# Half slots of a routed expert layer: layer 1 as products of 480 and 240 columns, with its sums, casts and low parts staggered by a block

## The chip, the cores and the metric

The kernel runs on one core of one Trainium2 chip. The metric is device time in microseconds (us). Three runs of the kernel before took 746.63 to 747.06 us, the median is 746.89 us. The core's engines each work through a queue of their own: TensorE (PE, products), ScalarE (ACT), VectorE (DVE), GpSimd (POOL, here mostly indirect DMAs) and SyncE (SP, which issues the other DMAs). PSUM, where PE puts its sums, has eight banks of 512 columns.

## The reference, cut to what matters

The first part is attention with a sigmoid; the change does not touch it. The second part is a layer of eight experts, each token going to one of them:

```python
logits = x @ w_gate
e_idx = np.argmax(logits, axis=1)
...
for e in range(E):
    mask = e_idx == e
    h = np.maximum(x[mask] @ w1[e], 0.0)
    ye = h @ w2[e]
    out[mask] = gate_w[mask, None] * eom[mask, e, None] * ye
```

There are 3,584 tokens (N) of 768 values, w1 is 768 x 1,024 and w2 is 1,024 x 768 for each expert.

## The kernel before, in words

Attention runs first (`attention`), and its last third already prepares the experts. Then the tokens are worked through in *slots*, one expert to a slot. A full slot holds 448 tokens (TB), a half slot up to 240 (TM), for what is left of an expert. How many of each there are is known only when the kernel runs, so the later slots stand in branches. In the runs shown seven full slots and two half slots are done; the two half slots are the last work of the kernel.

Numbers are kept in float32 and split into a high part, which the cast to PE's format gives (`split`, ScalarE), and a low part, the difference (VectorE): x into xh and xl, w1 into wh and wl, w2 into w2h and w2l, h into hh and hl. Each product of two matrices is three products of parts: high by high, high by low, low by high.

A half slot (`slot` with n = 32 * 8, which is not TB) goes like this.

- *Layer 1* (`layer1`, `layer1_mm`) has eight blocks, f = 0 to 7, of 128 rows of h. In each, PE makes six triples of products (d = 0 to 5), every one of 240 columns: wh by xh, wh by xl, wl by xh (lines 467 to 469). All three add into one PSUM bank of `psh`, three banks in turn. Then ScalarE takes the ReLU as hh (line 496), and VectorE the low part hl (line 497).
- Beside layer 1, w2 is split (`split_w2`, blocks 1 to 4, two rows of 128 x 768 a time), and as w2 and w1 share the raw buffer `w1r`/`w2r`, the loads of the next expert's w1 follow it (`load_w1`, SP). The next slot's tokens are gathered by GpSimd (`gather_rows`, line 389), one gather a block.
- *Layer 2* (`layer2`) has four groups of 24 products of 384 columns (lines 518 to 520): i = 0 and 1 make the two halves of the first 128 tokens, in the tile `ys[0]`, i = 2 and 3 those of the other 112, in `ys[1]`. ScalarE scales a group's sums into the tile (line 525), and after i = 1 and i = 3 GpSimd scatters the tile's rows to `out` (`scatter`, line 562).
- Beside layer 2, the next slot's w1 is split in three pieces of 128 x 2,048 (`split_w1`), its x is transposed by VectorE (`turn_x`) and split (`split_x`), and its w2 loaded (`load_w2`, SP) into the place that w1's raw pieces leave.

The first half slot has more to do, as it follows a full slot, whose last two columns' sums still stand in PSUM (`self.left`). The generator `finish` takes care of them, a step at each `next`: it turns them back (`turn_back`, VectorE, lines 485, 486, 508), stores them by eight DMAs, loads the rows again as four tiles, scales these on ScalarE (line 555) and scatters them from GpSimd. So six scatters leave during the first half slot's layer 2: two tiles named plain, then ys[0], hb, rbuf, then ys[1].

What sets the order: each engine's queue holds its instructions in the order in which the code writes them down, and an instruction that waits holds up all behind it. Waits come from the tiles: whoever writes a tile waits for those that still read it, DMAs among them.

A full slot's products are 512, 384 and 448 columns wide (`products`): xh and xl lie side by side in `x2`, and the first product takes 64 columns of xl along with 448 of xh, into a bank 512 wide.

Of the kernel before, what the change touches and what calls it, by code (L numbers as in the profile page):

```python
# [12 lines left out]
AF = mybir.ActivationFunctionType  # L13
ALU = mybir.AluOpType
# [16 lines left out]
TB = 448  # L31
TM = 240
GB_, GM = TB // 32, -(-TM // 32)
# [19 lines left out]
def r32(ap):  # L53
    return ap.bitcast(F32)


class Kernel:
# [19 lines left out]
    def memory(self):  # L77
        self.rounded = self.pool("rounded").tile([128, ROUNDED // 4], F32R, name="rounded")
        self.plain = self.pool("plain").tile([128, PLAIN // 4], F32, name="plain")
        ps = self.pool("psum", space=PSUM).tile([128, 8, 512], F32, name="ps")  # L80
        self.ps_s = [ps[:, 0:2], ps[:, 2:4]]
        self.ps_o = [[ps[:, 4], ps[:, 5]], [ps[:, 6], ps[:, 7]]]
        self.ps_s2 = ps[:, 6:8]
        self.psh = [ps[:, i] for i in (0, 1, 2)]
        self.psy = [ps[:, i] for i in (4, 5, 3)]
        self.ps_step = ps[:, 3, 0:8]
        self.rot = {}
        self.beat = [None, None]
        self.hints = {2: [ET.Activation, ET.DVE, ET.Pool]}

        c = self.carve
        w = c(0, 3, 2, 2, DF)
        self.w1s = [[w[:, d // 2, a, d % 2] for d in range(6)] for a in range(2)]
        self.w1p = [[w[:, k, a] for k in range(3)] for a in range(2)]
        self.x2 = c(12 * DF * 4, 6, 2 * TB)
        self.xs = [self.x2[:, :, TB * i:TB * i + TB] for i in range(2)]
        self.slots_begun = 0

        self.w1r = c(0, 6, DF, dt=F32)
        self.w2r = c(0, 8, DM, dt=F32)  # L100
        self.xg = c(6 * DF * 4, GB_, Q4, dt=F32)
        self.xT = c(6 * DF * 4 + XG, 6, TB, dt=F32)
        self.yq = c(6 * DF * 4 + XG, GB_, Q4, dt=F32)
        self.xTm = c(6 * DF * 4 + XG, 6, 32 * GM, dt=F32)
        self.spare = c(6 * DF * 4 + GM * Q4 * 4, DM, dt=F32), c(6 * DF * 4 + XG + 6 * 32 * GM * 4, DM, dt=F32)
# [315 lines left out]
        self.split(self.w1r[:, d], self.w1s[0][d], self.w1s[1][d])  # L421

    def split_w2(self, k):
        for f in (2 * k, 2 * k + 1):
            h, l = (w[f // 6][:, f % 6].rearrange("p (c a x) -> p a c x", a=4, x=32) for w in (self.w2h, self.w2l))
            self.split(self.w2r[:, f].rearrange("p (a c x) -> p a c x", a=4, x=32), h, l)

    def w2_at(self, f, c):
        return self.w2h[f // 6][:, f % 6, c], self.w2l[f // 6][:, f % 6, c]
# [18 lines left out]

    def split_x(self, s, k):
        if s is not None:  # L450
            q, n = slice(2 * k, 2 * k + 2), 32 * s["lx"].shape[1]
            self.split((self.xT if n == TB else self.xTm)[:, q], self.xs[0][:, q, 0:n], self.xs[1][:, q, 0:n])

    def change_step(self, times=2):
        for _ in range(times):
            self.nc.tensor.matmul(self.ps_step, self.zero, self.zero[:, 0:8], start=True, stop=True)

    def layer1_mm(self, f, n):
        nc = self.nc
        ps = self.h_ps = self.take("h", self.psh)  # L460
        c = slice(128 * f, 128 * f + 128)
        (wh, wl), (xh, xl) = self.w1s, self.xs
        for d in range(6):
            if n == TB and self.joined:
                mm = self.products(ps, wh[d][:, c], wl[d][:, c], self.x2[:, d], d == 0, d == 5)
            else:
                nc.tensor.matmul(ps[:, 0:n], wh[d][:, c], xh[:, d, 0:n], start=(d == 0), stop=False)  # L467
                nc.tensor.matmul(ps[:, 0:n], wh[d][:, c], xl[:, d, 0:n], start=False, stop=False)  # L468
                mm = nc.tensor.matmul(ps[:, 0:n], wl[d][:, c], xh[:, d, 0:n], start=False, stop=(d == 5))  # L469
            if d == 2:  # L470
                self.beat[1] = mm.ins
# [16 lines left out]
    def layer1(self, f, n, begun=False):  # L488
        nc = self.nc
        if not begun:  # L490
            self.layer1_mm(f, n)
        if n == TB and self.joined:
            self.join(self.h_ps)
        ps = self.h_ps[:, 0:n]
        hh, hl = (h[:, f, 0:n] for h in self.hs)
        self.beat[0] = nc.scalar.activation(hh, ps, AF.Relu).ins  # L496
        nc.vector.scalar_tensor_tensor(hl, ps, 0.0, r32(hh), ALU.max, ALU.subtract)  # L497

    def layer2_turned(self, c):
        ps = self.take("y", self.psy)  # L500
        for f in range(8):
            wh, wl = self.w2_at(f, slice(128 * c, 128 * c + 128))
            self.products(ps, wh, wl, self.h2[:, f], f == 0, f == 7)
        return ps
# [65 lines left out]
    def slot(self, cur, nxt, side=None, begun=False, hint=None):  # L570
        nx = None
        if nxt is not None:
            nx, rows, sure = nxt() if callable(nxt) else nxt
            last = -(-nx["lx"].shape[1] // 2) - 1
        n = 32 * cur["lx"].shape[1]
        lag = 0 if self.left is not None or n == TB else 2
        fin = self.finish(n)
        next(fin, None)
        self.rot["y"] = 1
        for f in range(8):  # L580
            if begun and f == 1:
                self.change_step()
            self.layer1(f, TB if n == TB else TM, begun and f == 0)
            if nx is not None and n < TB:
                if f >= lag:
                    self.gather_rows(nx, f - lag, rows, 1)
                if f == 7 and lag == 0:
                    self.nc.gpsimd.drain()
            elif nx is not None and f <= last:
                self.gather_rows(nx, 2 * f, rows, 1)  # L590
                self.gather_rows(nx, 2 * f + 1, rows, 0)
                if f == last and not sure:
                    self.nc.gpsimd.drain()
            if f == 6 and n < TB:
                next(fin, None)
            if side is not None:
                next(side, None)
            if 1 <= f < 5:
                self.split_w2(f - 1)
                if f > 1:  # L600
                    self.load_w1(nx, f - 2)
        if lag == 0:
            for k in range(3):
                self.turn_x(nx, k)
        if n == TB:
            next(fin, None)
            self.layer2_columns(cur, nx, side, hint, fin)
            self.slots_begun += 1
            return nx
        ws = {0: (0, 1), 1: (2,)}  # L610
        for i in range(4):
            t = i // 2
            self.layer2(cur, t, i % 2, self.ys[t])
            if nx is not None:
                if lag and i == 0:
                    for g in range(8 - lag, 8):
                        self.gather_rows(nx, g, rows, g % 2)
                    self.nc.gpsimd.drain()  # L618
                for k in ws.get(i, ()):
                    self.split_w1(k)  # L620
                    for j in range(k, 4 if k == 2 else k + 1):
                        self.load_w2(nx, j)
                if lag and i == 0:
                    for k in range(3):
                        self.turn_x(nx, k)
                if i < 3:
                    self.split_x(nx, i)
            if i < 2:
                next(fin, None)
            if side is not None:  # L630
                next(side, None)
            if hint is not None and i == 1:
                self.tc.mark_branch_hint_location(hint, hint="LikelyTaken", engines=[ET.SP])
        return nx
# [342 lines left out]
```

## Time and profile before

| | |
|---|---|
| runs, median (lowest to highest) | 746.89 us (746.63 to 747.06) |
| the profiled execution: time | 748.09 us |
| the profiled execution: span | 746.3 us, granted clock 0.998 |
| PE busy | 738.2 us, 99% of the span |
| VectorE, ScalarE, GpSimd busy | 60%, 50%, 34% |
| first half slot's layer 1, from first product to layer 2 | 674.03 to 690.24 us |
| second half slot's layer 1 | 706.92 to 723.04 us |
| last product starts | 739.52 us |

How to read it: the span runs from the first to the last instruction of one execution; the execution's own time lies some 2 us above it. Times on a timeline are microseconds from the span's start. Busy shares are means over stages with different limits, and PE's products are pipelined, so that a busy PE need not be at its peak; a product's own duration overlaps the next one's, and what a product costs is the time from its start to the next one's. After a group of instructions, in brackets, stands how long the engine sat idle before it, and what ended that.

### The profile page before, as it was taken

What the parts mean: (1) busy time and instruction counts of PE and PEld (TensorE: products, weight loads), DVE (VectorE), ACT (ScalarE), POOL (GpSimd) and SP (SyncE); (2) the same over time, 40 slices, a digit from 0 to 9 for tenths busy, and PEclk for the clock granted to TensorE, in tenths of its full rate; (3) what the DMA queues carried; (4) which work ended last, traced back from release to release, by engine and by line L of the source; (5) the groups of instructions that cost most, each with busy time, mean ns of one, the idle gap of its engine ahead of it and who ended that gap; (6) DMA issues with size and microseconds to landing.
All of it is one profiled execution on the core that took longest, in us unless ns stands there. A gap on an engine that the chain in (4) does not pass through costs nothing. (4 is left out here: it accounts for less than half of the span.)

```text
span 746.3 us, 14692 instructions
## 1 busy us (share of the span) xinstructions
PE 738.2 (99%) x5576; PEld 543.0 (73%) x5576; DVE 449.8 (60%) x907; ACT 370.1 (50%) x437; POOL 250.3 (34%) x375
## 2 busy tenths in 40 slices
PE   9999999999999999999999999999999999999996
PEld 4334444444344369999999999999999999999996
DVE  1343863585777849936746746746655565656555
ACT  5666666566777734404514514514514333434644
POOL 5000130032354335247525315315225234233461
PEclk9999999999999999999999999999999999999999
DMA  9464656647595765367386386476386476576951
GB/s 307 138 194 148 195 138 192 195 119 209 179 325 178 213 138 178 127 163 214 118 293 217 123 273 216 132 267 208 142 274 184 176 243 205 187 247 191 322 198 46
DMA packets 90647, 145.76 MB, mean 195 GB/s; under 512 B 16738, under 2 KB 67298, under 8 KB 90560
## 3 DMA queue, kind: packets, MB, share of 16 engines
q1 hardware_dynamic: 79808, 119.22, 51.9%
q0 software_dynamic: 9680, 24.53, 9.4%
q10 hardware_dynamic: 1072, 0.92, 0.5%
q8 instruction: 46, 0.75, 0.4%
q14 instruction: 41, 0.34, 0.1%
HBM read 118.40 MB, written 32.62 MB: 202 GB/s over the span
## 5 line engine op out<-in xcount | busy, mean ns | idle before, releaser
L709 ACT ACTIVATE a<-ps,small 128x896 f32<-128x896 f32 x168 | 168.5, 1007 | 85.2 <-PE ps L707 83.0
L707 PE MATMUL ps<-q,k 64*64 64x448 f32 x1344 | 157.1, 540 | 0.0
L716 PE MATMUL ps<-a,v 64*64 64x448 f32 x1344 | 155.8, 536 | 0.0
L389 POOL DMA_INDIRECT plain<-x_dram,lxs x112 | 111.0, 991 | 132.3 <-ACT h L496 63.2
L496 ACT ACTIVATE h<-ps 128x448 fp32r<-128x448 f32 (+1 forms) x72 | 36.5, 506 | 206.7 <-DVE ps L486 129.9
L479 PE MATMUL ps<-h,w2h 128*128 128x512 f32 x336 | 130.7, 389 | 0.0
L481 PE MATMUL ps<-h,w2l 128*128 128x448 f32 x336 | 122.6, 365 | 0.0
L479 PE MATMUL ps<-rounded 128*128 128x512 f32 x288 | 112.0, 389 | 0.0
L480 PE MATMUL ps<-h,w2h 128*128 128x384 f32 x336 | 111.9, 333 | 0.0
L707 PEld LDWEIGHTS ps<-q,k 64*64 64x64 f32 x1344 | 49.9, 134 | 76.8 <-issue 70.0
L716 PEld LDWEIGHTS ps<-a,v 64*64 64x64 f32 x1344 | 50.6, 133 | 75.7 <-issue 72.1
L481 PE MATMUL ps<-rounded 128*128 128x448 f32 x288 | 105.1, 365 | 0.0
L415 DVE TENSOR_TENSOR rounded<-plain,rounded 128x2048 fp32r<-128x2048 f32 (+5 forms) x63 | 96.4, 1566 | 10.0 <-ACT rounded L414 8.9
L480 PE MATMUL ps<-rounded 128*128 128x384 f32 x288 | 95.9, 333 | 0.0
L414 ACT CAST rounded<-plain 128x2048 fp32r<-128x2048 f32 (+5 forms) x63 | 82.0, 1333 | 24.8 <-DVE plain L434 23.6
L485 DVE COPY hb<-ps 128x64 f32<-128x64 f32 x90 | 19.8, 220 | 103.3 <-PE ps L481 86.4
L562 POOL DMA_INDIRECT out<-y,lts x24 | 42.8, 1782 | 105.3 <-ACT y L555 102.3
L481 PEld LDWEIGHTS ps<-h,w2l 128*128 128x128 f32 x336 | 63.1, 188 | 13.2
L415 DVE TENSOR_TENSOR w2l<-plain,w2h 128x768 fp32r<-128x768 f32 x72 | 65.8, 954 | 3.4 <-ACT w2h L414 0.6
L497 DVE SCALAR_TENSOR_TENSOR h<-ps,h 128x448 fp32r<-128x448 f32 (+1 forms) x72 | 41.3, 574 | 42.6 <-ACT h L496 36.1
L480 PEld LDWEIGHTS ps<-h,w2h 128*128 128x128 f32 x336 | 63.1, 188 | 4.9
L479 PEld LDWEIGHTS ps<-h,w2h 128*128 128x128 f32 x336 | 63.1, 188 | 0.0
(164 smaller groups left out, 934.6 us busy)
## 6 DMA issues: line engine op xcount, KB each, us to landing
plain<-w SPq DMA_DIRECT2D x40, 768.0 KB
plain<-w SPq DMA_DIRECT2D x27, 1024.0 KB
k<-kT SPq DMA_DIRECT2D x23, 448.0 KB
q<-qT SPq DMA_DIRECT2D x23, 448.0 KB
x_dram<-xt SPq DMA_DIRECT2D x30, 336.0 KB
v<-vm SPq DMA_DIRECT2D x23, 384.0 KB
y<-y_dram SPq DMA_DIRECT2D x18, 384.0 KB
y_dram<-plain SPq DMA_DIRECT2D x28, 192.0 KB
```

Source lines behind the costliest of these rows:

```text
L389: self.paced(self.nc.gpsimd.indirect_dma_start(out=self.xg[:, g], out_offset=None, in_=x4, in_offset=bass.IndirectOffsetOnAxis(ap=s["lx"][ ...
L414: self.nc.scalar.copy(hi, raw)
L415: self.nc.vector.tensor_tensor(lo, raw, r32(hi), ALU.subtract)
L479: mm(ps, wh, both[:, 0:512], start=first, stop=False)
L480: mm(ps[:, 512 - TB:TB], wh, both[:, 512:2 * TB], start=False, stop=False)
L481: return mm(ps[:, 0:TB], wl, both[:, 0:TB], start=False, stop=last)
L496: self.beat[0] = nc.scalar.activation(hh, ps, AF.Relu).ins
L497: nc.vector.scalar_tensor_tensor(hl, ps, 0.0, r32(hh), ALU.max, ALU.subtract)
L562: i = self.nc.gpsimd.indirect_dma_start(out=self.out, out_offset=bass.IndirectOffsetOnAxis(ap=at, axis=0), in_=y, in_offset=None, bounds_c ...
L707: qk = nc.tensor.matmul(ps[half[h], j, 0:S], k[half[j], e, o:o + 64], q[half[j], e], start=True, stop=True)
L709: self.beat[0] = nc.scalar.activation(at[u % 3], ps[:, :, 0:S], AF.Sigmoid, bias=self.bias_s, scale=1.0 / math.sqrt(D)).ins
L716: nc.tensor.matmul(self.ps_o[e][h][half[j], 0:S], v[half[h], e, c, j], a[half[h], j], start=(i in ((0, 3 if h else 4)[e],)), stop=(i == (2 ...
```

## The change

In half slots xh and xl now lie side by side (`split_x` writes both into `x2`), and layer 1's triple of 240 columns becomes a pair: wh by both, 480 columns, into columns 0 to 479 of a bank, and wl by xh, 240 columns, into its first 240 (`layer1_mm`). In the first half slot x was laid out for a full slot, so there the 480 columns are two pieces of 240 (`apart`). The bank is one of five (`pshm`). The second 240 sums must be added to the first: ScalarE copies them out of the bank, into `ys[0]` and `ys[1]` in turn, and VectorE adds them in (`layer1_half`).

The order beside it is new: casts of w2 begin in block 0 and their subtractions follow a block later, as does each block's low part (`rest`); `finish` takes its first step after block 0's add; and w1's first split and w2's first load stand ahead of layer 2.

```diff
+        self.pshm = [ps[:, i] for i in (0, 1, 2, 6, 7)]
...
     def split_x(self, s, k):
         if s is not None:
-            q, n = slice(2 * k, 2 * k + 2), 32 * s["lx"].shape[1]
-            self.split((self.xT if n == TB else self.xTm)[:, q], self.xs[0][:, q, 0:n], self.xs[1][:, q, 0:n])
+            q = slice(2 * k, 2 * k + 2)
+            x = self.xT if s["lx"].shape[1] == GB_ else self.xTm[:, :, 0:TM]
+            n = x.shape[2]
+            self.split(x[:, q], self.x2[:, q, 0:n], self.x2[:, q, n:2 * n])
...
-    def layer1_mm(self, f, n):
+    def layer1_mm(self, f, n, apart=True):
         nc = self.nc
-        ps = self.h_ps = self.take("h", self.psh)
+        ps = self.h_ps = self.take("h", self.psh) if n == TB else self.take("hm", self.pshm)
...
-            if n == TB and self.joined:
+            if n == TM:
+                both, to = self.x2[:, d, 0:2 * n], ps[:, 0:2 * n]
+                if apart:
+                    both = self.x2[:, d].rearrange("p (a t) -> p a t", a=2)[:, :, 0:n]
+                    to = to.rearrange("p (a t) -> p a t", a=2)
+                nc.tensor.matmul(to, wh[d][:, c], both, start=(d == 0), stop=False)
+                mm = nc.tensor.matmul(ps[:, 0:n], wl[d][:, c], xh[:, d, 0:n], start=False, stop=(d == 5))
+            elif self.joined:
...
+    def layer1_half(self, apart, nx, fin):
+        nc = self.nc
+        rest = None
+        for f in range(8):
+            self.layer1_mm(f, TM, apart)
+            ps, other = self.h_ps[:, 0:TM], self.ys[f % 2][:, 0:TM]
+            hh, hl = (h[:, f, 0:TM] for h in self.hs)
+            nc.scalar.copy(other, self.h_ps[:, TM:2 * TM])
+            nc.vector.tensor_tensor(ps, ps, other, ALU.add)
+            if f == 0:
+                next(fin, None)
+            else:
+                rest()
+            if f < 4:
+                for raw, high, low in self.w2_rows(f):
+                    nc.scalar.copy(high, raw)
+            if 1 <= f < 5:
+                for raw, high, low in self.w2_rows(f - 1):
+                    nc.vector.tensor_tensor(low, raw, r32(high), ALU.subtract)
+                if f > 1:
+                    self.load_w1(nx, f - 2)
+            self.beat[0] = nc.scalar.activation(hh, ps, AF.Relu).ins
+            rest = lambda ps=ps, hh=hh, hl=hl: nc.vector.scalar_tensor_tensor(hl, ps, 0.0, r32(hh), ALU.max, ALU.subtract)
+            yield f
+        rest()
...
-        next(fin, None)
+        if n == TB:
+            next(fin, None)
         self.rot["y"] = 1
-        for f in range(8):
+        for f in range(8) if n == TB else self.layer1_half(self.left is not None, nx, fin):
...
-        ws = {0: (0, 1), 1: (2,)}
+        ws = {0: (1,), 1: (2,)}
+        if nx is not None:
+            self.split_w1(0)
+            self.load_w2(nx, 0)
```

`w2_rows` yields the two rows that `split_w2` splits.

How it moves instructions, at three places. The names in brackets are the semaphores that an instruction waits for; w2h_2638 and w2l_2640 are six of the eight rows of w2's parts, y_2642 is `ys[0]` and y_2643 is `ys[1]`. DMASW0 to DMASW7 are raised in turn by GpSimd's DMAs when their data has landed.

ScalarE, where the second half slot's layer 1 begins, before and then with the change:

```order
L937 COMPARE_AND_BRANCH
L496 ACTIVATE h<-ps 128x240 [waits PE_49,Activation_49] x2
L414 CAST w2h_2638<-plain 128x4x6x32 [waits DMAHW2_49,Activation_49]
L414 CAST w2h_2638<-plain 128x4x6x32 [waits Activation_49]
L496 ACTIVATE h<-ps 128x240 [waits PE_49,Activation_49]
```

```order
L982 COMPARE_AND_BRANCH
L520 COPY y_2642<-ps 128x240 [waits DMASW2_49,PE_49,Activation_49]
L528 CAST w2h_2638<-plain 128x4x6x32 [waits DMAHW2_49]
L528 CAST w2h_2638<-plain 128x4x6x32
L534 ACTIVATE h<-ps 128x240 [waits DVE_49]
L520 COPY y_2643<-ps 128x240 [waits DMASW5_49,PE_49,Activation_49]
L528 CAST w2h_2638<-plain 128x4x6x32 [waits DMAHW3_49]
```

The first instruction of a block is now the copy, and the first two copies wait for DMASW2 and DMASW5; the ReLU waits for VectorE's add instead of PE.

GpSimd at the end of the first half slot; these rows are the same in both kernels but for their lines (these are of the change):

```order
L602 DMA out<-plain,left 3584x768 [waits DMASW0_49,DVE_49,Activation_49]
L602 DMA out<-plain,left 3584x768 [waits DMASW1_49,DVE_49,Activation_49]
L602 DMA out<-y_2642,ltb 3584x768 [waits DMASW2_49,Activation_49,Pool_49]
L602 DMA out<-hb,left 3584x768 [waits DMASW3_49,Activation_49]
L602 DMA out<-rbuf,left 3584x768 [waits DMASW4_49,Activation_49]
L602 DMA out<-y_2643,ltb 3584x768 [waits DMASW5_49,Activation_49]
```

A DMA waits for the earlier use of the semaphore that it raises itself: the scatter of `ys[0]` raises DMASW2, that of `ys[1]` DMASW5.

ScalarE, where the first half slot's layer 1 ends, before and then with the change:

```order
L496 ACTIVATE h<-ps 128x240 [waits PE_49,Activation_49] x3
L525 ACTIVATE y_2642<-ps,ltb 128x3x4x32 [waits DMASW2_49,DMASW0_49,DMASW4_49,PE_49,DMASW6_49,Activation_49,Pool_49]
L414 CAST rounded<-plain 128x2048 [waits DMAHW3_49]
L414 CAST rounded<-plain 128x2048 [waits DMAHW4_49]
L414 CAST rounded<-plain 128x2x256 [waits DVE_49]
```

```order
L534 ACTIVATE h<-ps 128x240 [waits DVE_49]
L415 CAST rounded<-plain 128x2048 [waits DMAHW3_49]
L565 ACTIVATE y_2642<-ps,ltb 128x3x4x32 [waits PE_49,Activation_49,Pool_49]
L415 CAST rounded<-plain 128x2048 [waits DMAHW4_49]
L415 CAST rounded<-plain 128x2x240 [waits DVE_49]
```

The first cast of w1 (128x2048) now stands ahead of the scaling of layer 2's first group; the second stays behind it.

## Rows read from the trace of the kernel before

**Rows 1.** The page, part 1: busy us, share, instructions, by engine.

```profile
PE 738.2 (99%) x5576; PEld 543.0 (73%) x5576; DVE 449.8 (60%) x907; ACT 370.1 (50%) x437; POOL 250.3 (34%) x375
```

**Rows 2.** Timeline of PE, 660 to 740 us: start us, us, engine, line, operation.

```profile
660.11 0.39 PE L479 MATMUL ps<-h,w2h 128*128 128x512 f32 x1
...
672.71 0.39 PE L479 MATMUL ps<-h,w2h 128*128 128x512 f32 x1
...
674.03 0.35 PE L467 MATMUL ps<-rounded 128*128 128x240 f32 x1 [0.56 <-PEq L923]
...
690.24 0.34 PE L518 MATMUL ps<-w2h,h 128*128 128x384 f32 x1
...
706.92 0.27 PE L467 MATMUL ps<-rounded 128*128 128x240 f32 x1
...
723.04 0.34 PE L518 MATMUL ps<-w2h,h 128*128 128x384 f32 x1
...
727.21 0.33 PE L518 MATMUL ps<-w2h,h 128*128 128x384 f32 x1
...
739.52 0.34 PE L520 MATMUL ps<-w2h,h 128*128 128x384 f32 x1
```

**Rows 3.** Timeline of GpSimd: four of the six scatters, 700 to 712 us.

```profile
700.58 3.10 POOL L562 DMA_INDIRECT out<-plain,left  x1 [9.96 <-DVE rounded L415]
703.99 2.70 POOL L562 DMA_INDIRECT out<-plain,left  x1 [0.30 <-issue]
706.99 1.23 POOL L562 DMA_INDIRECT out<-y,ltb  x1 [0.30 <-issue]
...
711.04 0.97 POOL L562 DMA_INDIRECT out<-y,ltb  x1 [0.30 <-issue]
```

**Rows 4.** DMA queue q0 (GpSimd's): 707 to 718, 717 to 718; all queues 718 to 719.

```profile
q0 software_dynamic: 544, 2.28, 51.3%
...
q0 software_dynamic: 53, 0.11, 37.7%
...
DMA packets 0, 0.00 MB, mean 0 GB/s; under 512 B 0, under 2 KB 0, under 8 KB 0
```

**Rows 5.** Instructions by line and shape: busy us, mean ns, idle before.

```profile
L414 ACT CAST w2h<-plain 128x768 fp32r<-128x768 f32 x72 | 56.2, 832 | 0.5 <-DMA plain<-w 0.5
...
L497 DVE SCALAR_TENSOR_TENSOR h<-ps,h 128x240 fp32r<-128x240 f32 x16 | 6.4, 401 | 9.0 <-issue 5.1 <-ACT h L496 3.8
...
L496 ACT ACTIVATE h<-ps 128x240 fp32r<-128x240 f32 x16 | 5.9, 371 | 22.0 <-PE ps L469 10.0 <-DVE ps L486 9.7 <-DVE plain L508 1.6
```

**Rows 6.** Timeline of VectorE in layer 1 of both half slots.

```profile
675.88 0.22 DVE L485 COPY hb<-ps 128x64 f32<-128x64 f32 x1 [10.79 <-PE ps L469]
...
678.25 0.37 DVE L497 SCALAR_TENSOR_TENSOR h<-ps,h 128x240 fp32r<-128x240 f32 x1
...
714.28 0.40 DVE L497 SCALAR_TENSOR_TENSOR h<-ps,h 128x240 fp32r<-128x240 f32 x1
714.60 1.82 DVE L415 TENSOR_TENSOR w2l<-plain,w2h 128x768 fp32r<-128x768 f32 x2
716.33 0.40 DVE L497 SCALAR_TENSOR_TENSOR h<-ps,h 128x240 fp32r<-128x240 f32 x1
```

**Rows 7.** Timeline of VectorE in the first half slot's layer 2.

```profile
696.51 1.90 DVE L434 STREAM_TRANSPOSE plain<-plain 128x512 f32<-128x512 f32 x3 [5.20 <-DMA plain<-w]
698.33 8.08 DVE L415 TENSOR_TENSOR rounded<-plain,rounded 128x2048 fp32r<-128x2048 f32 x5
706.67 0.69 DVE L415 TENSOR_TENSOR rounded<-plain,rounded 128x512 fp32r<-128x512 f32 x1 [0.26 <-ACT rounded L414]
```

**Rows 8.** Timeline of ScalarE: w2's last two rows, second half slot.

```profile
718.12 1.58 ACT L414 CAST w2h<-plain 128x768 fp32r<-128x768 f32 x2 [0.49 <-DMA plain<-w]
```

**Rows 9.** Stretches: length, busy us (x instructions) of five engines, PEclk, DMA share, GB/s.

```profile
739.00:743.00 4.00, 0.86 (x5) 0.54 (x4) 2.54 (x3) 1.06 (x2) 0.96 (x1) 1.00 0.24 66
743.00:744.00 1.00, 0.00 (x0) 0.00 (x0) 0.00 (x0) 0.00 (x0) 0.00 (x0) 0.53 0.31 119
```

More of the change, by code (lines that the diff above doesn't have):

```diff
@@ L423, in split_w2, with w2_rows @@
     def split_w2(self, k):
+        for raw, high, low in self.w2_rows(k):
+            self.split(raw, high, low)
+    def w2_rows(self, k):
         for f in (2 * k, 2 * k + 1):
             h, l = (w[f // 6][:, f % 6].rearrange("p (c a x) -> p a c x", a=4, x=32) for w in (self.w2h, self.w2l))
-            self.split(self.w2r[:, f].rearrange("p (a c x) -> p a c x", a=4, x=32), h, l)
+            yield self.w2r[:, f].rearrange("p (a c x) -> p a c x", a=4, x=32), h, l
     def w2_at(self, f, c):
@@ L577, in slot @@
         fin = self.finish(n)
-        next(fin, None)
+        if n == TB:
+            next(fin, None)
         self.rot["y"] = 1
-        for f in range(8):
+        for f in range(8) if n == TB else self.layer1_half(self.left is not None, nx, fin):
             if begun and f == 1:
                 self.change_step()
-            self.layer1(f, TB if n == TB else TM, begun and f == 0)
+            if n == TB:
+                self.layer1(f, n, begun and f == 0)
             if nx is not None and n < TB:
@@ L597, in slot @@
                 next(side, None)
-            if 1 <= f < 5:
+            if n == TB and 1 <= f < 5:
                 self.split_w2(f - 1)
```

## The prediction, made before the changed kernel ran

> **What bounds the kernel now.** I read the page's busy times first, then TensorE's (PE's) timeline over the last 90 us, then the timelines of the engines beside it there. PE is busy 99% of the span [rows 1], so time is won only by giving PE less, and lost wherever PE is made to wait. The change touches the half slots alone. Two of them run: in [rows 2] the first one's layer 1 begins at 674.03 and its layer 2 at 690.24, the second one's at 706.92 and 723.04, and the last product starts at 739.52. Between these rows PE never stands; the other engines all have slack here, and what the change asks is whether they keep it. Two facts decide. First, how GpSimd's scatters run at the seam between the half slots: six go out from 700.58 to 712.01, the one of ys[0] at 706.99, the one of ys[1] last, at 711.04 [rows 3]. Second, when their data has left: GpSimd's DMA queue moves 2.28 MB from 707 to 718, still 0.11 MB in its last microsecond, and after 718 nothing moves [rows 4]. So ys[1], last of the six, is free at about 717.5 to 718.
>
> **The change, part by part.** *Products.* Per block of layer 1 (f, eight per half slot) six triples of 240 columns become six pairs of 480 and 240. A 240-column product costs (723.04 - 706.92) / 144 = 111.9 ns from start to start; a triple of 512, 384 and 448 columns, 1,344 in all, costs (672.71 - 660.11) / 21 = 600 ns (21 triples lie between these rows) [rows 2]. A fixed part a and a slope b through both: 3a + 1344b = 600 and a + 240b = 111.9 give b = 0.424 ns a column and a = 10.2 ns. 480 columns then take 213.6 ns, a pair 325.5, a triple now 335.7: 10.2 ns saved, 0.49 us per half slot, **0.98 us** in all. Bounds: the 480 priced like 512 columns (227 ns) loses 0.3 us, priced without any fixed part (203 ns) gains 2.0 us. I take the line, since 480 lies between measured widths. The Trainium skill's page "TensorE: Matmul & The Clock Gate", section "Back-to-back issue gap", gives a fixed part of about 2.5 ns for an isolated product; by that the gain would be 0.24 us. The rows show four times as much here, and the sum goes by the rows.
>
> *New work on ScalarE and VectorE.* Each block gets a copy of 240 sums on ScalarE and an add of 240 on VectorE. The trace has neither; nearest are the 240-column ReLU (371 ns) and low part (401 ns), both out of PSUM [rows 5]; lower bound nothing, upper 0.45 us each. VectorE's present cycle in blocks 1 to 4 is 716.33 - 714.28 = 2.05 us [rows 6]; with the add (0.34 us, overlap as between those rows) it is 2.4, against PE's new block of 6 x 325.5 ns = 1.95 us. ScalarE's cycle of copy, two casts (832 ns each) and ReLU is about 2.1. So both fall behind, by 0.45 us a block over four blocks, under 2 us; five PSUM banks let PE run five blocks ahead. The first half slot, on VectorE: block 0's add ends near 677.1; the turning back takes 678.25 - 675.88 = 2.4 [rows 6], to 679.5; four cycles of 2.4, to 689.1; then the add of block 5 and block 4's low part, and two rounds of ReLU, copy and add with ScalarE at 1.15 each; the last low part comes at about 692.7. Layer 2 begins at 690.24 - 0.49 = 689.75 and takes eight steps of 0.52, three products each; the eighth wants that part at 689.75 + 7 x 0.52 + 0.34 = 693.7. Cost there: nothing, with 1 us to spare.
>
> *Moved.* finish's turning back now stands behind block 0's add, so its eight stores leave SP about 1 us later, and w1's three loads behind them. w1's first cast moves ahead of layer 2 on ScalarE, but the subtraction that follows it stays behind the three transposes on VectorE, which today wait until 696.51 for DMA and then run with the subtractions to 706.4 without a gap; the last one ends at 707.36 [rows 7]. The second half slot would want it at 706.43 + 4 x 0.3255 = 707.7. If DMA is 1 us later, PE stands there up to 0.8 us; I put 0 in the sum, because the next wait swallows it.
>
> *The wait that is added.* The copies go to ys[0] and ys[1] in turn. In the second half slot these are the tiles that the first half slot's scatters are still reading: the order on ScalarE shows copy 0 waiting for DMASW2 and copy 1 for DMASW5, the semaphores of those two scatters, and the order on GpSimd is as before. Before, nothing touched ys until layer 2. Copy 1 can start at T = 718.0 (by rows 3 and 4), though PE has block 1 ready at 710.5. Behind it in ScalarE's queue stand the casts of w2 and every ReLU; VectorE waits for the copy, PE for a bank. From T: copy and add 0.8; then VectorE is the bound: block 0's low part and two w2 subtractions 2.1, three more cycles of 2.4, then the add of block 5 and low part of block 4 0.7, two rounds of ReLU, copy and add between ScalarE and VectorE at 1.15 each, the last ReLU, low part and product 0.85. Layer 2's first group ends at T + 13.9 = 731.9. Block 5 starts at T + 1.2 = 719.2 instead of 716.2: 3 us in which PE stands, and it stands again, shortly, before blocks 6 and 7 and in the group. Today the second group starts at 727.21 [rows 2]. What follows is unchanged, 12.4 us of products and the tail, so the sum is 731.9 - 727.2 = **+4.7 us**; the 0.98 us gained are inside it.
>
> **Sum.** The profiled execution took 748.09 us (span 746.3), 1.2 above the median of the runs, 746.89. 748.09 + 4.7 = 752.8; on the median, 746.89 + 4.6 to 4.7 = **751.5 us**. Bounds of T: if the two long scatters (3.10 and 2.70 us) took 0.97 like the last one [rows 3], ys[1] would leave 3.9 us earlier, T = 714.1, +0.8 us; if the seam runs 1 us later because of w1's loads, T = 719, +5.7 us. I take 718, since GpSimd's order and VectorE's subtractions beside it are the same. The Trainium skill's page "SBUF — State Buffer", section "SBUF: two separate sides", says that GpSimd cannot write its DMA descriptors while VectorE holds the port that they share; the trace agrees, since the two long scatters lie beside VectorE's subtractions [rows 3, 7]. By that rule, were w1 really subtracted before the scatters, the sum would be +0.8; queued behind the transposes, it stays +4.7.
>
> **Rivals.** About 0.2%, 1.5 us, is what a measurement of this kernel can tell from no change.
> (1) *The wait as above*, T from 714.9 to 719: 748.5 to 752.5; chance 0.74.
> (2) *The scatters leave in time*, T below 711: PE gains its 0.98 us, minus what VectorE's cycle costs where w2's last rows land at 718.1 [rows 8]: cast, 1.8 us of subtractions and the catching up hold the first group 0.3 to 0.7 us. 746.2 to 746.6, on the faster side. For it: ys[0]'s scatter needs only 1.2 us of GpSimd; against: the five scatters ahead of ys[1]'s in the same queue. It decides at T = 713.3, where +0. Chance 0.06; over 0.2% faster needs the 480 at its lower bound too.
> (3) *The wait shrinks*, T from 711 to 714.9, because w1's earlier cast lets the seam run sooner: 746.5 to 748.4. For it: ScalarE's casts of w1 stand ahead of the first scatter's scaling, and one of them now comes earlier; against: that scaling also waits for y from memory, which leaves later now. Chance 0.11.
> (4) *The clock falls too.* After the last product, at 739.9, the granted clock stays at 1.00 until 743 and is 0.53 in the microsecond after, so near half, the 1.2 GHz level [rows 9]. PE had stood since its last product. Whether the stand before block 5 brings the same, the trace does not show. At 1.2 GHz blocks 5 and 6 would take 3.9 us instead of the 2.4 that VectorE sets: +1.5 us each, 753.0 to 755. Chance 0.09.
> (5) The change may also not do what it says in the first half slot, where the 480 columns are read and written as two pieces of 240: priced as two products it gives back 0.49 us, inside every range above.
>
> **The numbers.** Forecast 751.5. The range takes (1) whole, the upper half of (3) and the lower half of (4): 747.9 to 753.6. Slower by over 0.2% is (1) and (4): 0.83. Within 0.2% is (2) and (3) nearly whole: 0.14. Faster: 0.03.
>
> **What would show it.** Right: in the second half slot ScalarE's first two copies wait for the scatter of out, the second until about 718; PE waits some 3 us before its sixth block; layer 2 begins near 726; the first half slot has no stand in layer 1 and its pair is 325 ns. Wrong: copies that start when PE's block ends, PE at 99% with layer 2 at 722 (rival 2); a stand at block 5 well under 3 us (rival 3); a granted clock of 0.50 in a row before 735 (rival 4); PE waiting for VectorE in the first half slot, which I hold covered.

## The result, and the profile after

Six runs of the changed kernel took 750.09 to 752.26 us, median **751.62 us**; six of the kernel before, the three known at the time of the prediction and three beside the change, 747.16 us. The ratio, with its 95% interval, is **1.0057 [1.0047, 1.0068]**: slower by 4.3 us (0.0057 x 747.2), where 751.5 us was forecast.

The profiled execution took 750.49 us, span 748.7. Everything ahead of the half slots, which the change doesn't touch, happened to come 1.7 us earlier in it than in the profile of before (672.30 against 674.03 at the first half slot's first product). So the two are compared from that product to the end of the span: 748.7 - 672.30 = 76.40 us now, 746.3 - 674.03 = 72.27 before [rows 2], **+4.13 us**. PE's timeline after, beside [rows 2]:

```profile
672.30 0.45 PE L476 MATMUL ps<-rounded 128*128 128x480 f32 x1 [0.56 <-PEq L968]
...
672.70 0.38 PE L476 MATMUL ps<-rounded 128*128 128x480 f32 x1
...
687.73 0.38 PE L476 MATMUL ps<-rounded 128*128 128x480 f32 x1
...
704.72 0.38 PE L476 MATMUL ps<-rounded 128*128 128x480 f32 x1
...
714.19 0.38 PE L476 MATMUL ps<-rounded 128*128 128x480 f32 x1
714.41 0.27 PE L477 MATMUL ps<-rounded 128*128 128x240 f32 x1
717.33 0.57 PE L476 MATMUL ps<-rounded 128*128 128x480 f32 x1 [2.65 <-DVE h L535]
...
717.90 0.61 PE L476 MATMUL ps<-rounded 128*128 128x480 f32 x1
...
718.51 0.61 PE L476 MATMUL ps<-rounded 128*128 128x480 f32 x1
...
724.88 0.34 PE L558 MATMUL ps<-w2h,h 128*128 128x384 f32 x1
...
728.90 0.44 PE L560 MATMUL ps<-w2h,h 128*128 128x384 f32 x1 [0.31 <-DVE h L535]
...
729.73 0.33 PE L558 MATMUL ps<-w2h,h 128*128 128x384 f32 x1
```

The first half slot runs without a stand, pair behind pair: (687.73 - 672.70) / 46 = 326.7 ns, and the second one's first 30 pairs alike, (714.19 - 704.72) / 29 = 326.6 ns. Then PE stands 2.65 us before its sixth block, and the second group of layer 2 starts at 729.73, which is 57.43 us after the first half slot's start, against 53.18 before [rows 2]: the whole loss is there by then. The bracket names VectorE. What VectorE waited for stands on ScalarE's timeline, and what that waited for on GpSimd's:

```profile
710.97 0.36 ACT L520 COPY y<-ps 128x240 f32<-128x240 f32 x1 [5.40 <-DMA out<-y,ltb]
711.22 1.57 ACT L528 CAST w2h<-plain 128x768 fp32r<-128x768 f32 x2
712.69 0.37 ACT L534 ACTIVATE h<-ps 128x240 fp32r<-128x240 f32 x1
716.07 0.36 ACT L520 COPY y<-ps 128x240 f32<-128x240 f32 x1 [3.00 <-DMA out<-y,ltb]
```

```profile
702.43 2.73 POOL L602 DMA_INDIRECT out<-y,ltb  x1 [0.30 <-issue]
...
708.17 0.97 POOL L602 DMA_INDIRECT out<-y,ltb  x1 [0.30 <-issue]
```

GpSimd was done with ys[1]'s scatter at 709.14 (708.17 + 0.97); the copy that overwrites ys[1] was let go 6.9 us later, at 716.07. That is T, 43.77 us after the first half slot's start. VectorE's pace behind it:

```profile
716.46 0.42 DVE L521 TENSOR_TENSOR ps<-ps,y 128x240 f32<-128x240 f32 x1 [4.68 <-ACT y L520]
716.78 0.40 DVE L535 SCALAR_TENSOR_TENSOR h<-ps,h 128x240 fp32r<-128x240 f32 x1
717.10 1.82 DVE L531 TENSOR_TENSOR w2l<-plain,w2h 128x768 fp32r<-128x768 f32 x2
718.83 0.41 DVE L521 TENSOR_TENSOR ps<-ps,y 128x240 f32<-128x240 f32 x1
...
728.45 0.94 DVE L535 SCALAR_TENSOR_TENSOR h<-ps,h 128x240 fp32r<-128x240 f32 x2
```

One block takes 718.83 - 716.46 = 2.37 us. And the stretches around the stand (length, then busy us and instructions of PE, PE's weight loads, VectorE, ScalarE, GpSimd, then granted clock, DMA share, GB/s):

```profile
716.00:717.00 1.00, 0.00 (x0) 0.00 (x0) 0.54 (x2) 0.93 (x2) 0.00 (x0) 1.00 0.12 43
717.00:718.00 1.00, 0.67 (x3) 0.63 (x4) 1.00 (x3) 1.00 (x3) 0.00 (x0) 0.76 0.00 0
718.00:720.00 2.00, 2.00 (x8) 1.79 (x8) 2.00 (x5) 2.00 (x5) 0.40 (x1) 0.50 0.00 0
720.00:722.00 2.00, 2.00 (x11) 1.78 (x11) 2.00 (x5) 2.00 (x6) 1.23 (x1) 0.77 0.04 11
722.00:724.00 2.00, 2.00 (x14) 1.83 (x14) 2.00 (x4) 0.39 (x2) 1.23 (x1) 1.00 0.14 42
```

The granted clock fell to 0.50, the 1.2 GHz level, behind the stand and came back by 722. There a pair takes 0.61 us (718.51 - 717.90) in place of 0.33. Whether that cost time is one of the questions below.

### The profile page after: what moved, and what is told of

The parts are those of the page before. It is cut to its first block, busy times and chain, and to the rows that moved or that the text cites. A ratio compares the mean times of both kernels' runs of the same rounds, so it can differ in the third digit from the quotient of the medians.

```text
span 748.7 us, 14515 instructions
## 1 busy us (share of the span) xinstructions
PE 737.9 (99%) x5480; PEld 550.0 (73%) x5480; DVE 454.6 (61%) x923; ACT 374.4 (50%) x453; POOL 251.8 (34%) x375
## 5 line engine op out<-in xcount | busy, mean ns | idle before, releaser
L761 PE MATMUL ps<-a,v 64*64 64x448 f32 x1344 | 158.2, 536 | 0.0
L510 ACT ACTIVATE h<-ps 128x448 fp32r<-128x448 f32 x56 | 30.5, 545 | 187.0 <-DVE ps L500 164.9
L761 PEld LDWEIGHTS ps<-a,v 64*64 64x64 f32 x1344 | 55.3, 133 | 70.9 <-issue 67.4
L752 PEld LDWEIGHTS ps<-q,k 64*64 64x64 f32 x1344 | 54.8, 133 | 70.8 <-issue 66.1
L495 PEld LDWEIGHTS ps<-rounded 128*128 128x128 f32 x288 | 54.1, 188 | 11.1
L255 POOL TENSOR_TENSOR meta<-eom,den 64x1 f32<-64x1 f32 (+1 forms) x40 | 8.4, 209 | 150.8 <-DVE eom L252 149.0
```

The costliest lines, as they stand in the source:

```text
L495: return mm(ps[:, 0:TB], wl, both[:, 0:TB], start=False, stop=last)
L752: qk = nc.tensor.matmul(ps[half[h], j, 0:S], k[half[j], e, o:o + 64], q[half[j], e], start=True, stop=True)
L761: nc.tensor.matmul(self.ps_o[e][h][half[j], 0:S], v[half[h], e, c, j], a[half[h], j], start=(i in ((0, 3 if h else 4)[e],)), stop=(i == (2 ...
```

## The experiments

The theory: the copies wait until the scatters' data has left ys, and from T on a fixed chain through VectorE leads to the end. Rival A: VectorE's work per block (2.37 us against PE's 1.96) costs the time with or without the wait. Rival B: the fall of the clock does. Rival C: w1's earlier split does. "First product to end" is the page's span minus the start of the first half slot's first product; T is the start of block 1's copy in the second half slot, counted from the same product, where that copy, or block 0's ahead of it, waited for a scatter. Ratios are to the kernel before, timed beside each group of runs; its median was 746.89 us beside e1, e2, e3, e5, 748.04 beside e4, e6, e7, 748.46 beside e8 to e10 and 746.98 beside e11, e12, so each time is set only against the one beside it.

| kernel | first product | T after it | first product to end | ratio of runs |
|---|---|---|---|---|
| before | 674.03 | | 72.27 | |
| the change | 672.30 | 43.77 | 76.40 | 1.0057 [1.0047, 1.0068] |
| e1 own places | 672.98 | | 72.02 | 1.0000 [0.9991, 1.0009] |
| e2 ys[0] only | 672.61 | 40.21 | 72.89 | 1.0029 [1.0020, 1.0038] |
| e3 w1 ahead alone | 672.65 | | 72.15 | 1.0002 [0.9993, 1.0011] |
| e4 own places, no stagger | 674.09 | | 76.01 | 1.0068 [1.0054, 1.0081] |
| e5 PE kept busy | 673.05 | 44.29 | 76.95 | 1.0053 [1.0040, 1.0066] |
| e6 e1 with later casts | 674.63 | | 71.27 | 0.9999 [0.9990, 1.0008] |
| e7 ys[1] only | 674.17 | 45.19 | 77.83 | 1.0104 [1.0089, 1.0119] |
| e8 before again | 674.18 | | 72.12 | 1.0005 [0.9996, 1.0014] |
| e9 e6 again | 673.74 | | 72.06 | 0.9996 [0.9987, 1.0005] |
| e10 e6, w1 not ahead | 675.95 | | 71.65 | 1.0002 [0.9993, 1.0011] |
| e11 e6, split before turn | 672.66 | | 71.84 | 0.9990 [0.9981, 0.9999] |
| e12 e1, split before turn | 672.56 | | 71.74 | 0.9990 [0.9981, 0.9999] |

**e1, take away what makes the copies wait.** Other places, the wait gone:

```diff
+        self.others = c(6 * DF * 4 + 12 * Q4 * 4, TM, dt=F32), c(6 * DF * 4 + XG + (6 * 32 * GM + DM) * 4, TM, dt=F32)
-            ps, other = self.h_ps[:, 0:TM], self.ys[f % 2][:, 0:TM]
+            other = (self.ys if apart else self.others)[f % 2][:, 0:TM]
```

> The change with one difference: the copies of the second half slot's blocks go to two free stretches of SBUF that no scatter reads, in place of ys[0] and ys[1]. Theory (the wait for the scatters' data): ScalarE's copies L520 lose their waits of 5.4 and 3.0 us, TensorE its stand of 2.65 us before block 5, and what is left is the products' saving, 96 triples by 9.0 ns = 0.86 us: 0.3 to 1.0 us below the kernel before, 746.2 to 746.9 us. Rival A (the work per block: VectorE's 2.36 us a block against TensorE's 1.96 us sets the end with or without the wait): 750 us or more, near the changed kernel. Rival B (the granted clock, 0.50 over 3 us after the stand): it would keep its 1.00 here as well, so this run parts only A from the theory.

The whole loss goes: 747.14 us beside 746.89, ratio 1.0000. That refutes A; VectorE's work per block is the same here, 2.37 us where it sets the pace (719.74 to 722.11). But the saving is not seen either: 72.02 is 0.25 below 72.27 where 0.86 was due. ScalarE's and PE's timelines tell where it stayed:

```profile
717.62 1.57 ACT L530 CAST w2h<-plain 128x768 fp32r<-128x768 f32 x2 [2.64 <-DMA plain<-w]
```

```profile
725.09 0.44 PE L562 MATMUL ps<-w2h,h 128*128 128x384 f32 x1 [0.31 <-DVE h L537]
```

The next wait in the same queue: w2's last rows land at 717.6, their cast waits 2.64 us for them, block 4's copy stands behind that cast, and PE stands 0.65 us from start to start (724.44 to 725.09) in layer 2's first group. Before, too, that cast waited for its load, 0.49 us until 718.12 [rows 8].

**e2 and e7, the dose.** In e2 every copy goes to ys[0], free early; in e7 those of the second half slot go to ys[1], free last:

```diff
-            ps, other = self.h_ps[:, 0:TM], self.ys[f % 2][:, 0:TM]
+            ps, other = self.h_ps[:, 0:TM], self.ys[0][:, 0:TM]
```

```diff
+            ps, other = self.h_ps[:, 0:TM], (self.ys[f % 2] if apart else self.ys[1])[:, 0:TM]
```

> The change with every block's copy in ys[0] alone. In the changed kernel the copy into ys[0] was let go at 710.97 and the one into ys[1] at 716.07. Theory (the wait): one wait only is left, that of block 0 until about 711; block 1 follows about 1.5 us behind it in place of 716.1, so most of the loss goes, and some stays, since 712.5 lies near the point from which a wait costs: 0.4 to 2 us above the kernel before, 747.5 to 749.2 us, with one ScalarE wait for a DMA of about 5 us and no second one. Rival A (the work per block): a single place makes the copies wait for the sums as well, so 751 us or more. Rival B (the granted clock): without a stand of TensorE no fall, and the same as the theory.

> The change with every copy of the second half slot in ys[1], whose scatter left last: the copy into it was let go at 716.07 in the changed kernel. Theory (the wait; the end hangs on when block 1's sum can start): block 0's copy, its two casts and its ReLU then stand behind that wait as well, 2.0 us (copy to copy in ScalarE's queue) between block 0's copy and block 1's, so the end is 2.0 us later than with the change: 752.9 to 754.2 us. Rival A (work per block, not the wait): no change, 751 to 752 us.

ScalarE in e2, then in e7:

```profile
710.83 0.36 ACT L520 COPY y<-ps 128x240 f32<-128x240 f32 x1 [5.02 <-DMA out<-y,ltb]
...
712.82 0.36 ACT L520 COPY y<-ps 128x240 f32<-128x240 f32 x1
```

```profile
717.38 0.36 ACT L520 COPY y<-ps 128x240 f32<-128x240 f32 x1 [10.00 <-DMA out<-y,ltb]
...
719.36 0.36 ACT L520 COPY y<-ps 128x240 f32<-128x240 f32 x1
```

Each has its one wait, and block 1's copy 1.98 to 1.99 us behind it. Over the four kernels in which a copy waits, "first product to end" minus T is 32.63 (the change), 32.66 (e5), 32.68 (e2) and 32.64 us (e7), while T itself moves by 5 us: from T on, the end is fixed, and over this range T costs one for one. Carried on, the line meets the 72.27 of before at T = 39.6: that is where the kernel would break even, not where the wait begins to cost, as part of the products' saving is spent by then. The runs lost more than these profiles show (medians: e2 2.1 us above its kernel before, where the profiles give 0.6; e7 7.3, the top of what was expected, where they give 5.6), and e2's spread more: 746.58 to 750.37 us, against 746.22 to 747.95 for the kernel before. Only one execution of each was profiled, and it was among the fastest (747.33 us in e2, 753.88 in e7, the lowest there); that T, which hangs on when the scatters' data leaves, came later in the others is likely, not shown.

**e3, the last part of the change alone.**

```diff
-        ws = {0: (0, 1), 1: (2,)}
+        ws = {0: (1,), 1: (2,)}
+        if nx is not None:
+            self.split_w1(0)
+            self.load_w2(nx, 0)
```

> The kernel before with the last part of the change alone: the first part of w1's split and the first load of w2 are issued ahead of layer 2 in place of behind its first group. Theory (the wait for the scatters): this part costs and gains nothing, within 0.4 us of the kernel before, 746.8 to 747.6 us. Rival C (the earlier split takes VectorE's and ScalarE's time from layer 2 of the first half slot, or loads that collide with the scatters): 748 to 751 us.

746.85 beside 746.89 us: nothing, and C falls.

**e5, hold the clock.** PE gets something to do where it stands; the zeros add to nothing that is read:

```diff
+            if f == 5 and not apart:
+                for _ in range(28):
+                    nc.tensor.matmul(self.ps[:, 3, 0:128], self.zero, self.zero, start=True, stop=True)
```

> The change with 28 products of 128 columns of zeros ahead of block 5 of the second half slot, where TensorE stands for 2.65 us; their bank isn't in use then. TensorE is busy through most of the stand, so the granted clock should hold at 1.00 in 716 to 722. Theory (the wait; behind it VectorE's 2.36 us a block sets the pace, so a slower TensorE has time to spare): the same as the changed kernel, 750.9 to 752.2 us. Rival B (the granted clock's fall to 0.50 is what costs): 1.5 to 3 us less, 748.5 to 750.2 us.

```profile
717.00:718.00 1.00, 0.26 (x5) 0.09 (x2) 0.27 (x1) 0.66 (x2) 0.00 (x0) 1.00 0.07 22
718.00:720.00 2.00, 1.40 (x9) 1.31 (x10) 2.00 (x4) 2.00 (x5) 0.00 (x0) 1.00 0.00 0
720.00:722.00 2.00, 1.85 (x12) 1.47 (x11) 2.00 (x5) 2.00 (x5) 0.95 (x1) 1.00 0.06 16
```

The clock held at 1.00 throughout, and the time stayed: 751.40 us, 1.0053 against 1.0057, and from T to the end 32.66 us against 32.63. So the fall cost nothing, and B falls. PE is four blocks ahead of VectorE there: block 5's sum is taken at the earliest when VectorE has got through block 4's, 2.37 us a block.

**e4, undo the stagger, with own places.**

```diff
-            if f == 0:
-                next(fin, None)
-            else:
-                rest()
...
+            self.beat[0] = nc.scalar.activation(hh, ps, AF.Relu).ins
+            nc.vector.scalar_tensor_tensor(hl, ps, 0.0, r32(hh), ALU.max, ALU.subtract)
+            yield f
+            if 1 <= f < 5:
+                self.split_w2(f - 1)
```

> As the run with its own places for the copies (747.14 us, no wait for the scatters), and the stagger by a block undone: copy, sum, ReLU and low part of a block one behind the other, w2's rows cast and subtracted a block later as in the kernel before. It asks what the stagger is worth. If VectorE's chain matters (a block is then sum 0.32, hand-over and ReLU 0.40, low part 0.40, then the first cast piece 0.8 behind the ReLU and two subtractions 1.75: 3.0 to 3.4 us a block against 2.36 staggered, four blocks in each half slot, 2.6 to 4 us later at the last low part against about 1 us of slack): 748.5 to 752 us, with TensorE stands ahead of the last products of a first group of layer 2. If VectorE has room to spare: 747.2 us, within 0.5 us.

```profile
686.34 0.41 DVE L523 TENSOR_TENSOR ps<-ps,y 128x240 f32<-128x240 f32 x1
...
689.65 0.41 DVE L523 TENSOR_TENSOR ps<-ps,y 128x240 f32<-128x240 f32 x1
```

```profile
693.83 0.44 PE L553 MATMUL ps<-w2h,h 128*128 128x384 f32 x1 [1.19 <-ACT h L526]
695.00 0.44 PE L553 MATMUL ps<-w2h,h 128*128 128x384 f32 x1 [0.28 <-ACT h L526]
696.16 0.44 PE L553 MATMUL ps<-w2h,h 128*128 128x384 f32 x1 [0.28 <-ACT h L526]
```

A block takes VectorE 3.31 us (689.65 - 686.34) in place of 2.37, and PE stands in layer 2 of the first half slot, where the change has no stand. Ratio 1.0068: without the stagger the joined products cost some 4 to 5 us (76.01 against e1's 72.02 in the profiles, 0.0068 in the runs) even with no scatter in the way.

**e6 and e9, the next wait.** e1 with w2's casts and subtractions two blocks later in the second half slot:

```diff
+            j = f if apart else f - 2
-            if f < 4:
-                for raw, high, low in self.w2_rows(f):
+            if 0 <= j < 4:
+                for raw, high, low in self.w2_rows(j):
```

> As the run with its own places, and in the second half slot w2's casts stand two blocks later in ScalarE's queue (blocks 2 to 5 in place of 0 to 3), their subtractions likewise. With its own places the copies' wait was gone, but the cast of w2's last rows waited 2.64 us for their load until 717.62, and copy, sum and ReLU of block 4 stood behind it in ScalarE's queue; TensorE stood 0.65 us at the end of layer 2's first group, and the saving of 0.86 us was not seen. Theory (that load is the next wait, in the same queue): the stand goes and 0.5 to 0.9 us of the products' saving shows, 745.9 to 746.5 us. Rival (the load isn't what eats the saving): as with its own places, 746.8 to 747.4 us.

> The kernel with its own places and later casts again. Its profile gave 71.23 us from the first half slot's first product to the end, 1.04 less than before, but its runs were 0.9999 [0.999, 1.0008] of before: the two don't fit well. If the profile is right (all the products' saving shows, and the stretch ahead of the half slots, which this kernel doesn't change, took a random 0.5 to 1 us more in the timed runs): 0.4 to 1.1 us below the kernel before, ratio 0.9985 to 0.9995. If something of the changed program costs in the stretch ahead of the half slots: ratio 0.9995 to 1.001, and the first half slot starts 0.7 to 1.2 us later than in the kernel before on this chip.

In e6's profile no engine in layer 1 or 2 of the second half slot keeps PE waiting, and first product to end is 71.27 (e9's text has 71.23, and 72.12 for e3's 72.15), 0.85 to 1.00 us below the three profiles with the order of before (72.27, 72.15, 72.12): the 0.86 us of the products. Its runs didn't show it (748.01 beside 748.04), nor did those of the repeat clearly (747.78 beside 748.46, 0.9996 [0.9987, 1.0005]). The repeat's first half slot didn't begin later than that of before on the same chip (673.74 against 674.18 in e8), but its profile has 72.06, and a stand at the seam:

```profile
706.16 0.38 PE L477 MATMUL ps<-rounded 128*128 128x480 f32 x1
...
707.31 0.45 PE L477 MATMUL ps<-rounded 128*128 128x480 f32 x1 [0.34 <-DVE rounded L417]
...
708.21 0.45 PE L477 MATMUL ps<-rounded 128*128 128x480 f32 x1
...
708.61 0.38 PE L477 MATMUL ps<-rounded 128*128 128x480 f32 x1
```

The second half slot's products wait for VectorE's low parts of w1 and x, 0.61 us from start to start at the third pair, and the first five pairs take 708.61 - 706.16 = 2.45 us in place of 5 x 0.327 = 1.63: 0.82 us lost, as much as parts e9's profile from e6's (0.79). VectorE's last split of x, in e6 and then in e9:

```profile
707.14 0.66 DVE L417 TENSOR_TENSOR rounded<-plain,rounded 128x480 fp32r<-128x480 f32 x1 [0.24 <-ACT rounded L416]
```

```profile
707.40 0.66 DVE L417 TENSOR_TENSOR rounded<-plain,rounded 128x480 fp32r<-128x480 f32 x1 [0.24 <-ACT rounded L416]
```

From the first half slot's first product it ends after 33.17 us in e6 (707.80 - 674.63) and after 34.32 in e9 (708.06 - 673.74), the same kernel; in the kernel before after 33.33 [rows 2, 7]. So the seam moves by over 1 us from one execution to the next, and PE now reaches it 0.43 us earlier (48 pairs of 9.0 ns). The fifth pair is what needs that split: in e9 it starts 0.15 us behind its end (708.06 to 708.21). Counted from the second half slot's first product, the split ends after 0.75 us in e6 and 1.06 in the change, where no pair is slow; it ends after 1.13 in e10, 1.52 in e11, 1.64 in e12 and 1.90 in e9, and the first five pairs lose 0.05, 0.44, 0.55 and 0.82 us: what lies beyond 1.08 us is lost, one for one.

**e8, the kernel before again**, and **e10**, e6 with w1's split back behind layer 2's first group.

> The kernel before once more, unchanged, for its profile on the same chip as the next two runs, and for how far the comparison of equal kernels lies from 1. Expected of every theory: ratio within 0.001 of 1, and from the first product of the first half slot to the end 72.1 to 72.3 us, as in the two profiles with the order of before (72.27 and 72.12).

> The same with the last part of the change undone: w1's first split and w2's first load back behind layer 2's first group. Theory (nothing waits for them there): the tail as with them ahead, within 0.3 us of it. Rival (the earlier load of w2's first rows is what keeps the casts of the second half slot from waiting): a stand of TensorE or a ScalarE wait for w2's rows, and 0.5 to 1.5 us more.

e8: 1.0005 [0.9996, 1.0014] and 72.12, so equal kernels differ by up to 0.4 us here. e10: 71.65 and 1.0002 [0.9993, 1.0011], no stand and no wait for w2's rows; with or without the early split the runs are the same, as e3 had it.

**e11 and e12, relieve the seam.** w1's first split goes ahead of the transposes, into VectorE's wait for x; e11 on top of e6, e12 on top of e1:

```diff
+        ws = {0: (1,), 1: (2,)}
+        if n < TB and nx is not None:
+            self.split_w1(0)
+            self.load_w2(nx, 0)
         if lag == 0:
             for k in range(3):
                 self.turn_x(nx, k)
```

> The kernel with own places and later casts, and w1's first split put ahead of the transposes of x as well, into the 4 to 5 us in which VectorE waited ahead of them. In the repeated run of that kernel VectorE's last split of x ended at 707.4 to 708.1, TensorE stood 0.61 us at the seam between the half slots (its first product waited for a low part of L417), and the first half slot's saving of 0.44 us was gone again. Theory (the seam is the next bound, now that the first half slot is shorter): VectorE's chain ends 1 to 2 us earlier at the seam, no stand there, and 0.6 to 1.1 us of the products' saving shows: ratio 0.9985 to 0.9992. Rival (the loads set the seam, not VectorE's queue): no change, ratio 0.9993 to 1.0003.

> The kernel with its own places alone, its casts where the change has them, and w1's first split ahead of the transposes. Theory: no stand at the seam, but the cast that waits for w2's last rows, with the next copy behind it, stays, unless the splits' earlier end lets that load begin earlier: 0.3 to 0.9 us below the kernel before, ratio 0.9988 to 0.9996. Rival (neither matters): ratio 0.9996 to 1.0005.

```profile
692.23 2.29 DVE L417 TENSOR_TENSOR rounded<-plain,rounded 128x2048 fp32r<-128x2048 f32 x1 [1.38 <-ACT rounded L416]
...
702.85 2.86 DVE L417 TENSOR_TENSOR rounded<-plain,rounded 128x2048 fp32r<-128x2048 f32 x2 [3.53 <-ACT rounded L416]
705.95 0.66 DVE L417 TENSOR_TENSOR rounded<-plain,rounded 128x480 fp32r<-128x480 f32 x1 [0.24 <-ACT rounded L416]
```

```profile
705.09 0.38 PE L477 MATMUL ps<-rounded 128*128 128x480 f32 x1
...
707.16 0.39 PE L477 MATMUL ps<-rounded 128*128 128x480 f32 x1
```

Both took 746.2 us beside 746.98, 0.9990 [0.9981, 0.9999]: some **0.75 us below the kernel before**, the only ratios below 1 whose interval leaves out 1, if barely, and about 5 us below the change (0.0067 of the time). The reason given isn't borne out, though. In e11's rows (VectorE, then PE) the first subtraction does stand ahead now, but VectorE then waits 3.53 us for ScalarE's casts, and its last split ends 33.95 us after the first half slot's start (706.61 - 672.66), between e6 and e9 and not 1 to 2 us ahead of them. The casts in turn stand in ScalarE's queue behind the scaling of rows that `finish` loads again, which waited 1.03 and 0.76 us for those loads: that is nearer to the rival, that loads set the seam. So the seam still costs: five pairs in 707.16 - 705.09 = 2.07 us, 0.44 too many, and 0.55 in e12, where none was expected. e11's profile, 71.84, isn't below e6's 71.27 either, and both profiles are only 0.3 to 0.5 us below the three of before, so where the 0.75 us comes from, and what the swap itself is worth, stays open. The later casts aren't needed beside it: e12, without them, is equal, and its wait for w2's last rows has shrunk from 2.64 to 1.05 us. Together the runs without the wait that keep the stagger (e1, e6, e9 to e12) put the kernel between no gain and 0.75 us below before; the whole 0.86 us of the products shows in one profile, e6's.

## Why the prediction was right

The forecast was 751.5 us, 4.7 above before in the profile; measured are 751.62 us and 4.13. The mechanism came as forecast; that the times lie only 0.12 us apart is luck in part, since the kernel before came out at 747.16 us with the later runs and not at 746.89, and the loss at 4.3 in place of 4.6. The steps one by one:

- *The wait* is the cause: e1 takes it away and the 4.3 us with it, and e2 and e7 move the end as T moves. T came 43.77 us after the first half slot's start, forecast 718.0 - 674.03 = 43.97, and two errors cancel in that. GpSimd ended ys[1]'s scatter 36.84 us after that start (709.14 - 672.30), 1.14 sooner than before (712.01 - 674.03 = 37.98); and the data left 6.93 us behind it, not 6.0. The forecast also read T off the end of all traffic in GpSimd's queue, which holds the gathers of the next slot's tokens too, three of them from 707 to 718; that bounds T only from above. In the change the queue still moved 0.03 MB after T, in e7 0.11 MB after the copy was let go. The break-even point was put at T = 713.3, 39.3 after that start; the line above gives 39.6.
- *The chain from T* was put at 13.9 us to layer 2's second group and took 13.66 (716.07 to 729.73). With T 0.20 and the chain 0.24 shorter, and 0.12 less behind it (729.73 to 748.7 against 727.21 to 746.3), 4.7 becomes the 4.13 seen.
- *Products*: 0.98 us forecast, 335.7 - 326.7 = 9.0 ns a pair measured, 96 pairs, 0.86. The fixed part of a product carried over to 480 columns nearly whole; and the two pieces of 240 in the first half slot cost what 480 in one piece cost in the second, 326.7 and 326.6 ns, so rival (5) is out.
- *VectorE's cycle* 2.4 forecast, 2.37 measured; the first half slot was covered, as said: its last low part ended 18.2 us after the start (689.55 + 0.94 - 672.30; forecast 692.7 - 674.03 = 18.7). Without the stagger it wouldn't have been (e4); the prediction didn't price that.
- *Moved*: e3 shows the 0 of the sum. The seam cost nothing in the change's profile (704.72, 32.42 us after the start, as PE's products alone make it), but e9 shows that it is as tight as feared: 0.82 us lost there.
- *Rival (2)*, scatters that leave in time, was put at 0.3 to 0.7 us below before because w2's rows land late. e1 is that case: 0.25 us below in its profile, for that reason, and 0.0 in its runs, give or take 0.7.
- *Rival (4)* was wrong in its price. The clock did fall, as it allowed, to 0.50 behind the stand; but 1.5 us each for blocks 5 and 6 compared PE's slow block of 3.9 us with VectorE's 2.4 and left out that PE was four blocks ahead. Only block 5 ran slow, 3.62 us (717.33 to 720.95), and VectorE added its sums at 725.93, 5 us later. e5 puts the cost at nothing. The short stands forecast before blocks 6 and 7 show in e5 alone, 0.3 us each: at half clock PE comes to these blocks too late to stand.
- The Trainium skill's page "SBUF — State Buffer", section "SBUF: two separate sides": the trace after agrees with it as before, three scatters of 1.56 to 2.73 us beside VectorE's subtractions, one of 1.17 as these end, two of 0.92 and 0.97 behind them. As the prediction had it, the early cast didn't move the subtractions ahead of the scatters:

```profile
696.81 5.02 DVE L416 TENSOR_TENSOR rounded<-plain,rounded 128x2048 fp32r<-128x2048 f32 x3
702.02 2.86 DVE L416 TENSOR_TENSOR rounded<-plain,rounded 128x2048 fp32r<-128x2048 f32 x2 [0.19 <-ACT rounded L415]
```

```profile
698.40 1.56 POOL L602 DMA_INDIRECT out<-plain,left  x1 [9.94 <-ACT plain L595]
```

## What to carry to other kernels

A tile that is lent out as scratch must be free of its last reader, and the last reader of a scatter's source is the DMA, not the engine that issued it: find when its data has left, and set that against when the scratch is wanted. Behind such a wait look at what stands in the same engine's queue and follow it to the end; here the loss was one for one over the range that the runs cover, and the break-even point could be worked out from the profile of before. When a saving doesn't show after the large wait is gone, look for the next waits that the shorter stretch now meets: here a late load in the same queue, and then a seam that moves more from one profiled execution to the next than the saving is worth.

## What the runs showed of the hardware that was not expected

GpSimd's instruction for a scatter of ys[1] ended at 709.14 and the next write to the tile was let go at 716.07, 6.9 us later, in a stretch in which GpSimd's queue (q0) shared the DMA engines with SP's loads of w2 (q1). From 705 to 718 us the two moved (packets, MB, share of the engines):

```profile
q1 hardware_dynamic: 770, 2.22, 43.1%
q0 software_dynamic: 511, 1.98, 38.1%
```

And a clock at half speed over 3 us can cost nothing: the change ran so, e5 did not, and both took 751.4 to 751.6 us.
